# A decode step with a 65536-entry cache: the K and V chunks issued from another engine's queue

## The chip, the cores and the metric

The kernel runs on one core of a Trainium2 chip. The core has a matrix engine (TensorE, PE in the profile), a vector engine (VectorE, DVE), a scalar engine (ScalarE, ACT), GpSimd (POOL) and a sync engine (SyncE, SP) that mostly issues transfers. Sixteen DMA engines move data between HBM and the on-chip memory SBUF; PSUM holds TensorE's results. Engines wait for one another, and for transfers, through semaphores. The metric is device time in microseconds, as a median over runs; lower is better.

## What is computed

One token goes through a grouped-query attention block with a cache, and then a bilinear GLU. There are 32 query heads and 8 K/V heads, so four query heads share one K/V head. The cache has 65536 entries of 128 floats for each K/V head, once for K and once for V: 2 x 8 x 65536 x 128 floats of 4 bytes, 537 MB. Everything is float32.

```
q = layernorm(x) @ wq                       # (1, 32 x 128)
scores = q . k * 128**-0.5                  # per head, over 65536 entries
o = softmax(scores) . v
h = x + o @ wo                              # (1, 512)
n = layernorm(h)
out = h + ((n @ w_gate) * (n @ w_up)) @ w_down
```

## The kernel before

**Chunks.** The host lays K and V out as 64 chunks of 128 partitions x 16384 floats (8 MB each, `kvd[g]`). A K/V head has four K chunks and then four V chunks, so head h owns chunks 8h to 8h+7. SBUF has room for two: even chunks go into `kv[0]`, odd ones into `kv[1]`. The weights of a head (`wqo`: the query weights of the next head and the output weights of this one) have one buffer of their own, `wqo_sb`.

**TensorE.** `windows` multiplies a chunk in pieces of 512 columns (L364, 64 matmuls a chunk in the profile). It waits for the chunk's landing on a semaphore: `s_k0` for `kv[0]`, `s_v0` for `kv[1]`, each raised by 16 when a chunk has landed. The other semaphores of that kind (`s_k16`, `s_v8` and so on) exist for chunks that come in several pieces; GpSimd sets them to a high count at the start. When TensorE is done with a chunk it raises `kd`, and VectorE then raises `free` by one.

**SP's program.** All transfers of K, V and weights are issued by SP, in program order, on one queue. It loads the first query weights (L121), chunks 0 and 1, then chunks 2 to 5, each after taking one count of `free`. Then comes a loop over seven heads: take `wf` (VectorE says that the weights' buffer may be overwritten), issue the head's weights `wqo[h]` (L148), and then eight times take `free` and issue a chunk (`even`, L116, and `odd`, L119). After the loop come the last output weights `wo7` (L154), chunk 62, chunk 63 in four pieces (L160), and the GLU's weights (L163 to L172) into the two big buffers. The output is stored at L495.

**GpSimd** only prepares constants: an identity matrix, zeroed buffers, and the counts just named. Then it waits for the end of the program.

`take(e, s, n)` makes engine e wait until semaphore s has at least n and then takes n away.

```
    def even(g):
        sp.dma_start(kv[0], kvd[g]).then_inc(s_k0, 16)
    def odd(g):
        sp.dma_start(kv[1], kvd[g]).then_inc(s_v0, 16)
```

Of the kernel before, what the change touches and what calls it, by code (L numbers as in the profile page):

```python
# [13 lines left out]
NT = SK // CK  # L14
# [6 lines left out]
LAST = HKV - 1  # L21
PE_ONLY, DVE_ONLY, ACT_ONLY, SP_ONLY = (bass.OrderedEngineSet([e]) for e in (
    mybir.EngineType.PE, mybir.EngineType.DVE, mybir.EngineType.Activation, mybir.EngineType.SP))
# [7 lines left out]
class Counter:  # L31
# [5 lines left out]
    def tick(self, inst):  # L37
        self.n += 1
        inst.then_inc(self.sem, 1)
        return self.n  # L40


def body(nc, xr, kvd, wq0, wqo, wo7, gu, wd, out):
    pe_e, dve_e, act_e, pool_e, sp = nc.tensor, nc.vector, nc.scalar, nc.gpsimd, nc.sync

    def tile(name, *shape, align=32):
        return nc.alloc_sbuf_tensor(name, list(shape), F32, align_bytes=align).ap()
# [14 lines left out]
    kv = [tile(f"kv{i}", P, CK, align=1024) for i in range(2)]  # L62
    wqo_sb = tile("wqo_sb", P, 2, KT, 512, align=1024)
# [22 lines left out]
    def sem(name):  # L86
        sems.append(nc.alloc_semaphore(name))
        return sems[-1]
# [6 lines left out]
    pa, da, free, wf = (sem(n) for n in ("pa", "da", "free", "wf"))  # L95
    s_k0, s_k16, s_k24, s_k28 = (sem(f"s_k{i}") for i in (0, 16, 24, 28))
    s_v0, s_v8, s_v16, s_v24, s_v28 = (sem(f"s_v{i}") for i in (0, 8, 16, 24, 28))
    s_wq, s_w = sem("s_wq"), sem("s_w")
    s_wd = [sem(f"s_wd{i}") for i in range(NC - SIDE)]
    s_xr = sem("s_xr")  # L100
    late, s_act, s_pool, s_y, s_a, s_out = (sem(n) for n in ("late", "s_act", "s_pool", "s_y", "s_a", "s_out"))
    gu_t = kv[0].rearrange("p (k x) -> p k x", k=KT)[:, :, 0:2 * F]
    wd_t = kv[1]
# [2 lines left out]
    def take(e, s, n=1):  # L106
        e.wait_ge(s, n).then_inc(s, -n)  # L107
# [27 lines left out]
        pool_e.sem_inc(p, w * (end // 2 + n))  # L135
    for t in (o_pad, f_pad, sel_pad, acc, y):
        c_pads = pool.tick(pool_e.memset(t, 0.0))
    pool_e.wait_ge(s_act, 1).then_inc(s_pool, 1)
    pool_e.br("fin")

# [2 lines left out]
    for g in range(2, 6):  # L143
        take(sp, free)
        (odd if g % 2 else even)(g)
    with nc.Fori(0, LAST, engines=SP_ONLY) as h:
        take(sp, wf)
        sp.dma_start(wqo_sb, wqo[h]).then_inc(s_w, 16)  # L148
        with nc.Fori(0, 2 * NT, 2, engines=SP_ONLY) as c:
            for i, put in enumerate((even, odd)):  # L150
                take(sp, free)
                put(c + (h * (2 * NT) + 6 + i))
    take(sp, wf)
    sp.dma_start(wo_sb, wo7).then_inc(s_w, 16)  # L154
    take(sp, free)
# [175 lines left out]
    for o, g, u in ((f_pad[:, 0:1, 0], gux[0][:, 0, 3:4, 0], uf[:, 0, 1, 3:4, 0]),  # L331
                    (f_pad[:, 1:4, 0], gux[1][:, 1, 0:3, 0], uf[:, 1, 1, 0:3, 1]),
                    (f_pad[:, 4:5, 0], gux[1][:, 0, 3:4, 0], uf[:, 1, 1, 3:4, 0])):
        i = dve_e.scalar_tensor_tensor(
            out=o, in0=g, scalar=ln_r3[:, 0:1], in1=u, op0=ALU.mult, op1=ALU.mult)
# [17 lines left out]
    for k in range(KT):  # L353
        if k == KT - 1:
            pe_e.wait_ge(s_wq, 16)
        i = pe_e.transpose(ps[0][:, k:k + 1], xn_row[0:1, k * P:(k + 1) * P], ident[0:1, 0:1])
# [35 lines left out]
    for k in range(KT):  # L392
        i = mm(ptp[0][0:1, :], xn[:, k:k + 1], wq_sb[:, k, :], start=(k == 0), stop=(k == KT - 1))  # L393
    i.then_inc(pd, 1)
    pe_e.wait_ge(tok, 4)
    for r in range(REP):
        i = pe_e.transpose(sm[0][:, r:r + 1], qrow[0:1, r * P:(r + 1) * P], ident[0:1, 0:1])  # L397
# [13 lines left out]
    for half in range(2):  # L411
        pe_e.wait_ge(atok[half], 1)
        for b in range(4):
            i = pe_e.transpose(ptp[half][:, b * P:(b + 1) * P], ex[half][:, b * P:(b + 1) * P], ident)  # L414
# [9 lines left out]
    for half in range(2):  # L424
        step()
        for b in range(2):
            i = pe_e.transpose(ptp[half][:, b * P:(b + 1) * P],
                               gu_sb[:, (2 * half + b) * P:(2 * half + b + 1) * P], ident)
# [25 lines left out]
    for b in range(4):  # L454
        if b < 3:
            pe_e.wait_ge(*((tob, 1), (s_w, 16), (tob, 2))[b])
        i = pe_e.transpose(ptp[1][:, b * P:(b + 1) * P], orow[:, b * P:(b + 1) * P], ident)  # L457
    i.then_inc(pd, 1)
    pe_e.wait_ge(tok, 2)
    for r in range(REP):  # L460
        i = mm(attn[32 * r:32 * r + 32, :], o_pad[:, r, :], wo_sb[:, r, :],  # L461
               start=True, stop=True)
# [6 lines left out]
    for k in range(KT):  # L469
        if k % 2 == 0:  # L470
            pe_e.wait_ge(*((s_a, HKV) if k else (tok, 3)))
        i = pe_e.transpose(ptp[1][:, k * P:(k + 1) * P], acc[:, k * P:(k + 1) * P], ident)
# [69 lines left out]
```

## Time and profile before

| | |
|---|---|
| median of 3 runs | 1308.68 us (1308.65 to 1309.05) |
| span of the profiled execution, first to last instruction | 1307.4 us |
| median less that span | 1.3 us |
| TensorE matmuls, busy | 686.2 us (52%) |
| VectorE, busy | 111.6 us (9%) |
| ScalarE, busy | 54.9 us (4%) |
| GpSimd, busy | 2.7 us (12 instructions) |
| read from HBM | 564.66 MB |

The profile is of one execution. Busy times of different engines overlap, so they do not add up to the span. "Idle before" in a row is the time in which that engine stood still ahead of an instruction, with what ended the wait. Waiting and issuing a transfer are not counted as busy; a transfer's own time shows in the DMA rows. In a row of a timeline the first number is the start and the second the length, both in microseconds. PEld is the loading of weights into TensorE, and a name ending in q (SPq, DVEq) is an engine's instruction stream, where waits and issues stand.

### The profile page before, as it was taken

Reading aid. Unit: us, or ns where it says so; the run is one execution under the profiler, and the core shown is the slowest. Engines: PE = TensorE matmul, PEld = TensorE weight load, DVE = VectorE, ACT = ScalarE, POOL = GpSimd, SP = SyncE. Lnnn points to the kernel's source line nnn. Section 1 sums busy time; section 2 is a strip of 40 time slices with the busy share of each in tenths; the row PEclk is TensorE's granted clock in tenths of the full one; section 3 lists DMA queues with packets and bytes.
Section 4 is the critical chain, followed back from the end, with each engine's and each line's share of the span. In section 5 each row is a group of like instructions: output and inputs, shape, how many; then the busy total and the mean of one; then the engine's idle time right before and its main releaser. Section 6 shows DMA issues by size and latency. Waiting matters only on the chain. (4 is left out here: it accounts for less than half of the span.)

```text
span 1307.4 us, 10833 instructions
## 1 busy us (share of the span) xinstructions
PE 686.2 (52%) x4610; PEld 191.5 (15%) x4610; DVE 111.6 (9%) x286; ACT 54.9 (4%) x106; POOL 2.7 (0%) x12
## 2 busy tenths in 40 slices
PE   4456364453654545553554636535566445545557
PEld 1011111110111111111110211101111111111112
DVE  1000010100101001000010101001010010100101
ACT  0000000000000000000000000000000000000000
POOL 0000000000000000000000000000000000000000
PEclk8676796776976768767787767868677677877679
DMA  9999999999999999999999999999999999999999
GB/s 417 421 445 429 437 447 419 449 417 449 417 449 417 449 417 449 421 445 427 439 439 427 449 417 449 417 449 417 449 417 449 417 434 440 441 437 429 447 408 382
DMA packets 12850, 564.72 MB, mean 432 GB/s; under 512 B 1409, under 2 KB 1457, under 8 KB 2610
## 3 DMA queue, kind: packets, MB, share of 16 engines
q1 hardware_dynamic: 12848, 564.71, 99.8%
q10 hardware_dynamic: 2, 0.00, 0.0%
HBM read 564.66 MB, written 0.05 MB: 432 GB/s over the span
## 5 line engine op out<-in xcount | busy, mean ns | idle before, releaser
L364 PE MATMUL ps<-kv,st 128*32 128x512 f32 x4184 | 591.0, 728 | 534.6 <-DMA kv<-in_kv 520.1
L364 PEld LDWEIGHTS ps<-kv,st 128*32 128x32 f32 x4184 | 146.7, 131 | 962.3 <-DMA kv<-in_kv 568.1
L242 DVE TENSOR_REDUCE mx<-sc 128x1 f32<-128x512 f32 x32 | 21.9, 686 | 535.9 <-DVEq L107 535.9
L414 PE MATMUL ptp<-ident,ex 128*128 128x128 f32 x128 | 27.3, 372 | 19.8 <-ACT ex L220 19.5
L216 ACT COPY sc<-ps 128x512 f32<-128x512 f32 x32 | 18.8, 586 | 444.6 <-ACTq L107 444.5
L274 DVE TENSOR_TENSOR orow<-ps,orow 128x512 f32<-128x512 f32 x16 | 11.1, 691 | 298.3 <-DVEq L107 298.3
L220 ACT ACTIVATE ex<-sc,nbias 128x512 f32<-128x512 f32 x32 | 22.8, 714 | 304.4 <-ACTq L107 304.4
L393 PE MATMUL ptp<-wqo_sb,xn 128*1 128x512 f32 x64 | 30.4, 620 | 6.4 <-DVE acc L288 5.0
L216 ACT ACT_TABLE_LOAD x8 | 10.3, 1283 | 441.5 <-ACTq L107 441.5
L261 DVE COPY st<-ptp 128x512 f32<-128x512 f32 x32 | 22.1, 692 | 44.5 <-DVEq L107 44.5
L414 PEld LDWEIGHTS ptp<-ident,ex 128*128 128x128 f32 x128 | 20.2, 188 | 22.9 <-ACT ex L220 22.8
L407 PE MATMUL sm<-ident,m 128*1 128x128 f32 x16 | 4.5, 283 | 27.2 <-DVE m L244 17.6
L277 DVE TENSOR_TENSOR orow<-ps,orow 128x256 f32<-128x256 f32 x16 | 6.0, 419 | 129.3 <-DVEq L107 129.3
L272 DVE COPY orow<-ps 128x512 f32<-128x512 f32 x8 | 5.5, 692 | 102.0 <-DVEq L107 102.0
L461 PE MATMUL attn<-wqo_sb,o_pad 128*32 128x512 f32 x64 | 8.5, 605 | 5.9 <-DVE o_pad L284 5.9
L409 PE MATMUL sm<-ones,mexp 1*128 1x1 f32 x32 | 6.9, 281 | 6.7 <-DVE mexp L251 6.7
L393 PEld LDWEIGHTS ptp<-wqo_sb,xn 128*1 128x1 f32 x64 | 4.9, 85 | 30.9 <-issue 18.1
L224 DVE COPY qrow<-ptp 1x512 f32<-1x512 f32 x8 | 5.4, 679 | 29.7 <-DVEq L107 29.7
L457 PE MATMUL ptp<-ident,orow 128*128 128x128 f32 x32 | 6.1, 300 | 3.0 <-DVE orow L277 3.0
L407 PEld LDWEIGHTS sm<-ident,m 128*1 128x1 f32 x16 | 1.3, 79 | 41.8 <-DVE m L244 24.9
L288 DVE SCALAR_TENSOR_TENSOR acc<-attn,acc 128x256 f32<-128x256 f32 x16 | 6.2, 421 | 10.8 <-DVEq L107 10.8
L397 PE MATMUL sm<-ident,qrow 1*128 1x1 f32 x32 | 3.2, 201 | 7.1 <-DVE qrow L224 7.1
(84 smaller groups left out, 78.4 us busy)
## 6 DMA issues: line engine op xcount, KB each, us to landing
wqo_sb<-in_wqo SPq DMA_DIRECT2D x7, 2048.0 KB, 32.9
kv<-in_kv SPq DMA_DIRECT2D x1, 4096.0 KB, 22.2
kv<-in_gu SPq DMA_DIRECT2D x1, 3584.0 KB, 17.6
kv<-in_kv SPq DMA_DIRECT2D x1, 2048.0 KB, 26.7
kv<-in_kv SPq DMA_DIRECT2D x2, 1024.0 KB, 29.7
kv<-in_gu SPq DMA_DIRECT2D x1, 1792.0 KB, 21.4
kv<-in_wd SPq DMA_DIRECT2D x1, 1536.0 KB, 19.0
kv<-in_wd SPq DMA_DIRECT2D x5, 256.0 KB, 20.5
```

The source lines that it names most:

```text
L216: act_e.copy(sc[s], ps[s % 2]).then_inc(ad, 1)
L220: act_e.activation(ex[s - n], sc[s], AF.Exp, bias=nbias[:, 0:1], scale=SCALE, accum_out=sums[:, s:s + 1]).then_inc(atok[s - n], 1)
L242: dve_e.tensor_reduce(out=mx[:, s:s + 1], in_=sc[s], axis=AX.X, op=ALU.max).then_inc(own, 1)
L261: dve_e.tensor_copy(st[:, :, 0:16].rearrange("p g (b h) -> p b g h", h=REP), ptp[n % 2].rearrange("p (b g h) -> p b g h", b=4, h=REP)).the ...
L274: mine(dve_e.tensor_tensor(out=orow, in0=ps[n % 2], in1=orow, op=ALU.add))
L288: dve_e.scalar_tensor_tensor(out=acc[:, cs], in0=attn[:, cs], scalar=1.0, in1=acc[:, cs], op0=ALU.mult, op1=ALU.add, accum_out=rsum[:, hal ...
L364: i = mm(ps[buf][32 * j:32 * j + 32, :], st[:, 8 * j + r, :], kv[buf][:, w * 512:(w + 1) * 512], start=(r == 0), stop=(r in (2, 3, 7)), sk ...
L393: i = mm(ptp[0][0:1, :], xn[:, k:k + 1], wq_sb[:, k, :], start=(k == 0), stop=(k == KT - 1))
L409: mm(sm[0][:, 0:1], mexp.rearrange("p g h -> p (g h)"), ones[0:1, 0:1], start=True, stop=True).then_inc(pd, 1)
L414: i = pe_e.transpose(ptp[half][:, b * P:(b + 1) * P], ex[half][:, b * P:(b + 1) * P], ident)
L457: i = pe_e.transpose(ptp[1][:, b * P:(b + 1) * P], orow[:, b * P:(b + 1) * P], ident)
L461: i = mm(attn[32 * r:32 * r + 32, :], o_pad[:, r, :], wo_sb[:, r, :], start=True, stop=True)
```

## The change

Of the 64 chunks, numbers 6 to 61 are now issued by GpSimd in a loop of its own. GpSimd starts after SP has issued chunk 5 and raised a new semaphore `go`; it takes `free` before every chunk, as SP did. A chunk's landing no longer raises the semaphore on which TensorE waits: it raises `landed[0]` or `landed[1]`, and SP waits for that count and then raises `s_k0` or `s_v0` by 16 itself. SP's loop is written out in full, 56 steps long, with the weights `wqo[h]` issued at every eighth step. The last output weights, chunks 62 and 63 and the GLU's weights stay with SP, behind the 56 steps.

```
+POOL_ONLY = bass.OrderedEngineSet([mybir.EngineType.Pool])
...
+    go = sem("go")
+    landed = [sem(f"landed{i}") for i in range(2)]
...
         c_pads = pool.tick(pool_e.memset(t, 0.0))
+    take(pool_e, go)
+    with nc.Fori(0, LAST, engines=POOL_ONLY) as h:
+        with nc.Fori(0, 2 * NT, 2, engines=POOL_ONLY) as c:
+            for i, (buf, p) in enumerate(zip(kv, landed)):
+                take(pool_e, free)
+                pool_e.dma_start(buf, kvd[c + (h * (2 * NT) + 6 + i)]).then_inc(p, 16)
     pool_e.wait_ge(s_act, 1).then_inc(s_pool, 1)
...
     for g in range(2, 6):
         take(sp, free)
         (odd if g % 2 else even)(g)
-    with nc.Fori(0, LAST, engines=SP_ONLY) as h:
-        take(sp, wf)
-        sp.dma_start(wqo_sb, wqo[h]).then_inc(s_w, 16)
-        with nc.Fori(0, 2 * NT, 2, engines=SP_ONLY) as c:
-            for i, put in enumerate((even, odd)):
-                take(sp, free)
-                put(c + (h * (2 * NT) + 6 + i))
+    sp.sem_inc(go, 1)
+    for g in range(6, 2 * NT * LAST + 6):
+        n = (g - 6) // 2 + 1
+        if g % 8 == 6:
+            take(sp, wf)
+            sp.dma_start(wqo_sb, wqo[g // 8]).then_inc(s_w, 16)
+        sp.wait_ge(landed[g % 2], 16 * n)
+        sp.sem_inc(s_v0 if g % 2 else s_k0, 16)
     take(sp, wf)
     sp.dma_start(wo_sb, wo7).then_inc(s_w, 16)
```

Below, the rows of an engine's instruction stream give the code line, the operation and, in brackets, the semaphores for which it waits. First SP before the change, from the last two loads ahead of the loop to chunk 63 (the loop's body begins behind the two branches; what is left out is its second half and the jumps back):

```order
L116 DMA kv<-in_kv 128x16384 [waits free]
L119 DMA kv<-in_kv 128x16384 [waits free]
L146 UNCONDITIONAL_BRANCH
L148 ISA [waits wf]
L148 DMA wqo_sb<-in_wqo 128x4096
L149 UNCONDITIONAL_BRANCH
L116 ISA [waits free]
L116 DMA kv<-in_kv 128x16384
...
L154 DMA wqo_sb<-in_wo 128x2048 [waits wf]
L116 DMA kv<-in_kv 128x16384 [waits free]
L160 DMA kv<-in_kv 128x8192 [waits free]
```

The same place in SP's stream after the change (the lines are numbered anew; L162 is the former L148, L166 the former L154):

```order
L121 DMA kv<-in_kv 128x16384 [waits free]
L124 DMA kv<-in_kv 128x16384 [waits free]
L162 DMA wqo_sb<-in_wqo 128x4096 [waits wf]
L162 DMA wqo_sb<-in_wqo 128x4096 [waits landed0,landed1,wf] x6
L166 DMA wqo_sb<-in_wo 128x2048 [waits landed0,landed1,wf]
L121 DMA kv<-in_kv 128x16384 [waits free]
L172 DMA kv<-in_kv 128x8192 [waits free]
```

The loop's chunks are gone from SP. Its seven loads of `wqo` stand in a row; the first has no landing ahead of it, the other six, and the load of `wo7` at L166 with chunk 62 behind it, stand behind waits for landings. Now GpSimd's stream after the change, from its last memset to its last wait:

```order
L142 MEMSET y 128x256
L144 UNCONDITIONAL_BRANCH [waits go]
L145 UNCONDITIONAL_BRANCH
L148 ISA [waits free]
L148 DMA kv<-in_kv 128x16384
L148 ISA [waits free]
L148 DMA kv<-in_kv 128x16384
L145 REGISTER_ALU
L145 COMPARE_AND_BRANCH
L144 REGISTER_ALU
L144 COMPARE_AND_BRANCH
L150 UNCONDITIONAL_BRANCH [waits s_act]
```

Before, the last memset was followed at once by the wait for the end (`s_act`); now two nested loops with two chunks a turn stand between them, each chunk behind one count of `free`.

## What I expect, and why

> **What bounds the kernel now.** I read the queue table first, then one long stretch of the transfers, then the waits, and last the timeline where work changes hands.
>
> ```profile
> q1 hardware_dynamic: 12848, 564.71, 99.8%
> DMA packets 9552, 511.71 MB, mean 434 GB/s; under 512 B 1072, under 2 KB 1072, under 8 KB 1072
> PEld ps L364 <- DMA kv<-in_kv: 568.1, 63, 13.0
> SPq L107 <- SPq L107: 1225.3, 66, 32.5
> ```
>
> The first line is the page's: one queue carries all the data, and its packets fill 99.8% of the time of the sixteen DMA engines. The second is the stretch from 20 to 1200 us, at a steady 434 GB/s. A chunk of 128x16384 floats (8.39 MB) therefore takes 8.39/434 = 19.3 us. The other two are waits: TensorE waits 568 us for chunks, and the sync engine (SP) 1225 us, nearly all of it for free buffers. Compute has time to spare; the end is set by bytes and by any moment in which the DMA engines have nothing queued. There is almost none today, so the 0.2% that is left (2.6 us) is all that better queueing could win.
>
> ```profile
> 54.52 0.33 SPq L119 DMA_DIRECT2D kv<-in_kv  x1
> 44.26 9.96 PE L364 MATMUL ps<-kv,st 128*32 128x512 f32 x64 [9.95 <-DMA kv<-in_kv]
> 993.33 0.33 SPq L116 DMA_DIRECT2D kv<-in_kv  x1
> 1000.94 2.79 PE L364 MATMUL ps<-kv,st 128*32 128x512 f32 x12 [8.14 <-DMA kv<-in_kv]
> ```
>
> This is why the queue never empties. A chunk that TensorE takes up at 44.26 is worked through by 54.2, and the next load into its buffer is issued at 54.52. The chunk already in flight needs 19.3 us from 44, so the new one stands in the queue about 9 us before it is needed. The second pair shows the thinnest place that I found: the issue at 993.33, and the chunk ahead of it taken up at 1000.94. So every issue has a **cushion** of at least 7 us.
>
> **The change part by part.**
>
> *The relay.* SP now sees a landing and hands TensorE the count: 56 times one wait and one increment.
>
> ```profile
> L107 SPq EVENT_SEMAPHORE  x74: 17/17/17, 34.6 to 1307.4; - x74
> 1305.37 0.42 DVE L492 COPY y<-pva 64x256 f32<-64x256 f32 x1 [1.78 <-PE pva L374]
> 1305.81 0.36 SPq L495 DMA_DIRECT2D out_y<-y  x1
> ```
>
> SP's semaphore instructions take 17 ns, and SP issues the output within 0.1 us of the end of the copy that releases it. I take 0.1 us per chunk, between 0.03 us (two instructions) and 0.3 us (from TensorE's end at 54.22 through VectorE to SP's issue at 54.52, two steps, in the rows above). TensorE starts, and frees its buffer, that much later; the 7 us cushion hides it. Without the cushion it would cost 56 x 0.1 = 6 us.
>
> *GpSimd's issue.* Its queue never carried data before, so its time from free buffer to first byte has no row. Below it is bounded by nothing, above by the 2.4 us that a load into an empty queue costs (worked out below); I take 1 us. The cushion hides either end. GpSimd's older work ends with the memset below at 3.46 us, so nothing stands behind its new waits except its last step at the end of the program.
>
> ```profile
> 3.14 0.32 POOL L137 MEMSET y<- 128x256 f32 x1
> L234 DVE COPY st<-qx x8: 693/694/695, 16.5 to 1140.2; 128x1024 f32<-128x1024 f32 x8
> ```
>
> Eight VectorE copies from SBUF to SBUF take 0.69 us each. The Trainium skill (SBUF — State Buffer, "SBUF: two separate sides") warns that GpSimd cannot write a transfer's descriptors while such a copy holds the port that they share. By that rule an estimate of at most 8 x 0.69 = 5.5 us of late issues would be added; the cushion of 7 us makes it nothing, and no run here shows it yet.
>
> *The rate on GpSimd's queue.* Unknown. Below: no gain, since packets already stand back to back. Above: if each of the 56 chunks exposed its whole start, 56 x 2.4 = 134 us. Between these, if the queue cuts the 64 KB rows smaller, the tail of the trace has prices for it.
>
> ```profile
> DMA packets 160, 8.65 MB, mean 433 GB/s; under 512 B 16, under 2 KB 16, under 8 KB 16
> DMA packets 279, 1.60 MB, mean 422 GB/s; under 512 B 18, under 2 KB 18, under 8 KB 279
> DMA packets 491, 0.89 MB, mean 405 GB/s; under 512 B 56, under 2 KB 56, under 8 KB 491
> ```
>
> These are three stretches: 125 to 145 us (whole rows of K and V), 1295.2 to 1299 (pieces of 6 KB), 1301.3 to 1303.5 (2 KB). Beside each count stand the small completion packets. At 422 GB/s a chunk takes 19.9 us, 0.55 more, x56 = 31 us; at 405 GB/s 20.7, 1.4 more, 78 us. I take no loss, because the nearest row is the chunk itself, whose shape and addresses do not change.
>
> The Trainium skill (DMA: Bandwidth & Descriptors, "Bandwidth", the measured table) gives 425 GB/s for 16 MB issued from GpSimd. An estimate by that figure is 19.74 us a chunk, 0.4 more, and a total near 1335 us; no run here shows it yet.
>
> *The first handover, chunk 5 to chunk 6.* SP's queue still holds chunk 5 and, behind it, the weights of L148, issued at 93.38, when GpSimd issues chunk 6 at about 113 into a queue of its own. From there two queues share the engines.
>
> ```profile
> 93.38 0.35 SPq L148 DMA_DIRECT2D wqo_sb<-in_wqo  x1
> 112.79 0.34 SPq L116 DMA_DIRECT2D kv<-in_kv  x1
> 121.65 4.94 PE L364 MATMUL ps<-kv,st 128*32 128x512 f32 x25 [9.40 <-DMA kv<-in_kv]
> 130.97 0.33 SPq L119 DMA_DIRECT2D kv<-in_kv  x1
> 145.87 1.94 PE L364 MATMUL ps<-kv,st 128*32 128x512 f32 x8 [11.12 <-DMA kv<-in_kv]
> ```
>
> Chunk 5 has some 8 us of data left at 113. Shared evenly it lands near 129 instead of 121.3, and its buffer is free about 9.3 us after (121.65 to 130.97), near 139. Chunk 5, the weights and chunk 6 together still end at 145.5, so chunk 7 is issued in time: no cost. Sharing never creates bytes; it costs only if something then runs dry.
>
> *The weights of the later heads.* SP issues them only after the landing of the sixth of eight chunks, beside one that GpSimd has already queued. They take 2.10 MB/434 = 4.8 us of DMA time as before, and the head's end, which needs them, is still two chunks (over 38 us) away: no cost.
>
> *The last handover, chunk 61 to 62.* Here is the one term that I count. SP issues the last weights (L154) and then chunk 62, until now far ahead:
>
> ```profile
> 1209.71 0.34 SPq L154 DMA_DIRECT2D wqo_sb<-in_wo  x1
> 1228.65 0.34 SPq L116 DMA_DIRECT2D kv<-in_kv  x1
> 1237.59 6.77 PE L364 MATMUL ps<-kv,st 128*32 128x512 f32 x44 [9.26 <-DMA kv<-in_kv]
> 1259.42 3.63 PE L364 MATMUL ps<-kv,st 128*32 128x512 f32 x15 [8.62 <-DMA kv<-in_kv]
> ```
>
> Chunk 61 is taken up at 1237.59, chunk 62 at 1259.42. Before, both issues were made by 1229. Now SP stands in front of them waiting for chunk 61's landing, and everything behind that wait on SP (the weights, chunks 62 and 63, the GLU weights) is late. GpSimd has nothing more to issue, so all queues are empty at that landing. What a load into an empty queue costs, the first and the last one show:
>
> ```profile
> wqo_sb<-in_wq SPq DMA_DIRECT2D x1, 1024.0 KB, 4.8
> wqo_sb<-in_wo SPq DMA_DIRECT2D x1, 1024.0 KB, 30.3
> out_y<-y SPq DMA_DIRECT2D x1, 48.0 KB, 1.6
> ```
>
> The program's first load, 1024 KB, needs 4.8 us, of which 1.05 MB/434 = 2.4 is transfer: **2.4 us** of start and landing. The output, 48 KB, has 1.6 - 0.1 = 1.5 us. The load in question is the first one's size and also comes from HBM, so I take 2.4, with 1.5 as the lower end; SP's semaphore steps add 0.1, at most 0.3. All that follows is one chain of transfers to the end, so the whole of it, **2.5 us** (1.6 to 2.7), arrives there.
>
> ```profile
> span 1307.4 us, 10833 instructions
> 1280.60 18.98 DMA kv<-in_wd
> ```
>
> *Sum.* Span 1307.4 + 2.5 = 1309.9. The median of the runs, 1308.68, lies 1.3 above that span; with the same 1.3 around it the forecast is 1311.2 us, 0.19% slower. The chain's last transfer, the second line, only moves.
>
> **The rivals.**
>
> *GpSimd's queue is slower per chunk* (slower overall). Place: each of 56 chunks; price: 0.1 us each makes 5.6 us, 6 KB pieces 31 us, with the handover 1317 to 1342; at 2 KB pieces or an exposed start, up to 1445. It decides as soon as a chunk's time exceeds 19.3 us. For it: no row of before shows this queue moving data. Against it: the same rows, buffers and addresses, and 7 us in which an issue can be prepared. Chance 0.27, of which 0.07 lies above 1342. An extreme of it, a chunk at half the rate, would add 56 x 19.3 = 1081 us: 2392 us, chance 0.03. The microseconds column of the skill's measured table just named (79.0 for 16 MB) would mean about that, against its own GB/s column.
>
> *The queues share unevenly at the first handover* (slower). If chunk 6 goes first, chunk 5 lands at 121.3 + 19.3 = 140.6, its buffer is free at 150, and all queued data has ended at 145.5: idle from there to 150 plus about 2 us of start, 6.5 us, total 1317.7. It decides once chunk 5 lands after about 134. Nothing shows an order between queues; chance 0.06.
>
> *The last handover costs less, or the change does not do what it says* (same). If the next load starts almost at once, or some load is still queued at that landing, the total is 1308.7 to 1310. For it: SP reacts in 0.1 us. Against: even the tiny output needs 1.6 us. Chance 0.07; 0.02 of that I give to a gain past 0.2%, for which packets would have to run faster than 434 GB/s.
>
> **How the numbers follow.** The forecast (only the last handover counts, 1310.2 to 1312.5) has 0.57. The measurement tells about 0.2% from no change, so the border is 1311.3, and the forecast lies right on it: 0.33 below, 0.24 above. Same: 0.33 + 0.05 = 0.38; slower: 0.24 + 0.27 + 0.03 + 0.06 = 0.60; faster 0.02. The range runs from 1308.7 (a free handover) to 1342 (6 KB pieces), leaving out about 0.12; the forecast's own is 1310.2 to 1312.5.
>
> **What would show it.** In the queue table of the changed kernel a second queue carries about 56 x 8.39 = 470 MB; over the middle heads the rate stays 434 GB/s, and a chunk is taken up every 19.3 us. A lower rate there, or more packets than 128 a chunk, is the first rival. Chunk 5 is taken up near 129 instead of 121.65; after 134 is the second. After chunk 61's take-up a gap of about 2 us without packets stands before L166's weights, and chunk 62 is taken up 2.5 us later than 1259.42. Idle DMA stretches anywhere else, or a GpSimd issue less than 1 us before it is needed, would prove the cushion argument wrong.

## The result, and the profile after

The changed kernel takes **1311.81 us** (median of 11 runs, 1311.59 to 1312.03) against 1308.73 us for the kernel before (11 runs): ratio 1.0023, 95% interval 1.0014 to 1.0032. It is 3.1 us slower. The profiled execution has a span of 1310.7 us, 3.3 above that of before.

First the page of the changed kernel: its span, its queues, and the wait that took the place of TensorE's wait for transfers. Then the stretch from 20 to 1200 us.

```profile
span 1310.7 us, 10877 instructions
q0 software_dynamic: 8064, 469.77, 82.7%
q1 hardware_dynamic: 4784, 94.95, 16.9%
q14 instruction: 1, 0.01, 0.0%
PEld ps L376 <- SPq L164: 499.4, 55, 13.0
DMA packets 9553, 511.72 MB, mean 434 GB/s; under 512 B 1072, under 2 KB 1072, under 8 KB 1072
```

A second queue, q0, now carries 469.77 MB, which is the 56 chunks. The packets are as large and as many as before (9553 against 9552 in the same stretch), and the rate is the same 434 GB/s. The one packet more is on q14, an instruction fetch. TensorE now waits for SP's relay (L164) instead of the transfers, but hardly longer: 499.4/55 = 9.1 us a time, where before it was 568.1/63 = 9.0, and at most 13.0 as before.

The time is lost at the last handover. The timeline of the changed kernel shows TensorE taking up chunks 61 and 62, with SP's issues between them; the fifth line is the transfers of the stretch from 1237.75 to 1239.2, and the last line the weights' time from issue to landing.

```profile
1238.15 8.71 PE L376 MATMUL ps<-kv,st 128*32 128x512 f32 x64 [9.47 <-SPq L164]
1238.24 0.33 SPq L166 DMA_DIRECT2D wqo_sb<-in_wo  x1
1238.69 0.35 SPq L121 DMA_DIRECT2D kv<-in_kv  x1
1262.33 1.93 PE L376 MATMUL ps<-kv,st 128*32 128x512 f32 x8 [11.19 <-DMA kv<-in_kv]
DMA packets 3, 0.02 MB, mean 17 GB/s; under 512 B 0, under 2 KB 0, under 8 KB 0
wqo_sb<-in_wo SPq DMA_DIRECT2D x1, 1024.0 KB, 4.7
```

The weights, issued 30.3 us ahead of their landing before, now take 4.7 us: they start into an empty queue, and 1.45 us pass with 3 packets in them. From chunk 61 to chunk 62 it is 1262.33 - 1238.15 = 24.18 us; before it was 1259.42 - 1237.59 = 21.83. The difference is **2.35 us**.

Of all executions behind this document one, of the run early62 below, fell in a slow state (1425.69 us) and is left out of that run's ratio.

### The profile page after: what moved, and what is told of

Read it like the earlier page. It is cut to its first block, busy times and chain, and to the rows that moved or that the text cites. A ratio compares the mean times of both kernels' runs of the same rounds, so it can differ in the third digit from the quotient of the medians.

```text
span 1310.7 us, 10877 instructions
## 1 busy us (share of the span) xinstructions
PE 685.5 (52%) x4610; PEld 192.0 (15%) x4610; DVE 111.5 (9%) x286; ACT 54.9 (4%) x106; POOL 32.4 (2%) x68
## 3 DMA queue, kind: packets, MB, share of 16 engines
q0 software_dynamic: 8064, 469.77, 82.7%
## 5 line engine op out<-in xcount | busy, mean ns | idle before, releaser
L376 PE MATMUL ps<-kv,st 128*32 128x512 f32 x4184 | 589.4, 726 | 538.4 <-SPq L164 455.8
L376 PEld LDWEIGHTS ps<-kv,st 128*32 128x32 f32 x4184 | 146.2, 130 | 965.2 <-SPq L164 499.4
L148 POOL DMA_DIRECT2D kv<-in_kv x56 | 29.7, 530 | 1177.1 <-POOLq L112 1177.1
L426 PE MATMUL ptp<-ident,ex 128*128 128x128 f32 x128 | 28.5, 387 | 19.7 <-ACT ex L232 19.5
L273 DVE COPY st<-ptp 128x512 f32<-128x512 f32 x32 | 22.1, 692 | 45.2 <-DVEq L112 45.2
## 6 DMA issues: line engine op xcount, KB each, us to landing
kv<-in_gu SPq DMA_DIRECT2D x1, 1792.0 KB, 23.2
```

The lines of the kernel that those rows point to most:

```text
L148: pool_e.dma_start(buf, kvd[c + (h * (2 * NT) + 6 + i)]).then_inc(p, 16)
L273: dve_e.tensor_copy(st[:, :, 0:16].rearrange("p g (b h) -> p b g h", h=REP), ptp[n % 2].rearrange("p (b g h) -> p b g h", b=4, h=REP)).the ...
L376: i = mm(ps[buf][32 * j:32 * j + 32, :], st[:, 8 * j + r, :], kv[buf][:, w * 512:(w + 1) * 512], start=(r == 0), stop=(r in (2, 3, 7)), sk ...
```

## Experiments

All are edits of one of the two kernels; each was timed beside the kernel before on the same chip.

| run | median, us | before, us | ratio, 95% interval |
|---|---|---|---|
| early62 | 1309.10 | 1308.84 | 1.0003 (0.9994 to 1.0011) |
| sp_relay | 1308.86 | 1308.84 | 1.0001 (0.9992 to 1.0010) |
| slow_relay | 1400.15 | 1308.84 | 1.0694 (1.0679 to 1.0710) |
| slow_relay_8 | 1316.23 | 1308.77 | 1.0056 (1.0040 to 1.0073) |
| second_gap | 1316.05 | 1308.84 | 1.0055 (1.0042 to 1.0068) |
| pool_one_at_a_time | 1506.56 | 1308.77 | 1.1512 (1.1493 to 1.1531) |
| sp_one_at_a_time | 1483.56 | 1308.77 | 1.1335 (1.1316 to 1.1354) |

**Fill the queue at the last handover (early62).** The first line stands behind GpSimd's loop, the rest in SP's.

```
+    pool_e.sem_inc(gone, 1)
...
         if g % 8 == 6:
             take(sp, wf)
             sp.dma_start(wqo_sb, wqo[g // 8]).then_inc(s_w, 16)
+        if g == 2 * NT * LAST + 5:
+            take(sp, wf)
+            sp.dma_start(wo_sb, wo7).then_inc(s_w, 16)
+            take(sp, gone)
+            take(sp, free)
+            even(end - 2)
         sp.wait_ge(landed[g % 2], 16 * n)
         sp.sem_inc(s_v0 if g % 2 else s_k0, 16)
-    take(sp, wf)
-    sp.dma_start(wo_sb, wo7).then_inc(s_w, 16)
-    take(sp, free)
-    even(end - 2)
```

> The changed kernel, but SP issues the last output weights and chunk 62 before it waits for chunk 61's landing (GpSimd tells SP when its loop is done, so that SP takes the right count of `free`). Theory (the empty queue at the last handover is the cost, 2.4 us in the changed kernel's trace): 1311.8 - 2.4 = 1309.4 us, and chunk 62's data follows chunk 61's without a pause. Rival (the relay or GpSimd's queue costs a little on each of the 56 chunks): 1311.8 us, as the change.

Measured: 1309.10 us; 2.7 us of the 3.1 are gone, and the interval includes no difference from before. SP's timeline in this run shows the two issues far ahead of the landing, and TensorE's shows the take-ups of chunks 61 and 62:

```profile
1218.93 0.33 SPq L166 DMA_DIRECT2D wqo_sb<-in_wo  x1
1228.59 0.33 SPq L121 DMA_DIRECT2D kv<-in_kv  x1
1240.29 8.94 PE L379 MATMUL ps<-kv,st 128*32 128x512 f32 x64 [12.01 <-SPq L171]
1259.85 2.79 PE L379 MATMUL ps<-kv,st 128*32 128x512 f32 x12 [6.34 <-DMA kv<-in_kv]
```

Chunk 61 is taken up 2.1 us later than in the change (1240.29 after 1238.15): the last weights, issued by SP at 1218.93, now share the engines with it, and nearly all of their 2.4 us of transfer comes ahead of its landing instead of behind it. Chunk 62 is taken up at 1259.85, 0.4 us later than before the change instead of 2.9. Relay and GpSimd's queue are as in the change, so they are not the cost; the empty queue is.

**The relay alone (sp_relay).** SP issues every chunk as before, on its own queue.

```
-    for g in range(2, 6):
+    for g in range(2, 5):
         take(sp, free)
         (odd if g % 2 else even)(g)
+    take(sp, free)
+    sp.dma_start(kv[1], kvd[5]).then_inc(landed[1], 16)
...
+    def relay(i):
+        take(sp, landed[i], 16)
+        sp.sem_inc((s_k0, s_v0)[i], 16)
...
-            for i, put in enumerate((even, odd)):
+            for i in range(2):
                 take(sp, free)
-                put(c + (h * (2 * NT) + 6 + i))
+                sp.dma_start(kv[i], kvd[c + (h * (2 * NT) + 6 + i)]).then_inc(landed[i], 16)
+                relay(1 - i)
...
     even(end - 2)
+    relay(1)
```

> The kernel before with the relay alone: SP still issues every chunk, but chunks 5 to 61 raise a semaphore of SP's, and SP hands TensorE the count, always after it has issued the next chunk. No GpSimd queue, no empty queue. Theory (the relay is hidden by the cushion): 1308.7 to 1309.0 us. Rival (the relay is the cost): 1311.8 us.

Measured: 1308.86 us, no difference. A relay behind a filled queue costs nothing here.

**A longer relay (slow_relay, 24 turns; slow_relay_8, 8 turns).** A turn raises and takes a semaphore that nobody else uses.

```
         sp.wait_ge(landed[g % 2], 16 * n)
+        with nc.Fori(0, 24, engines=SP_ONLY):
+            sp.sem_inc(slack, 1)
+            take(sp, slack)
         sp.sem_inc(s_v0 if g % 2 else s_k0, 16)
```

> The changed kernel with each relay made longer: 24 turns of an empty loop on SP between the landing and the count, by estimate 2 to 4 us. Theory (hidden by the cushion of some 7 us; paid once, at the last handover, where nothing is queued): the change plus one delay, 1314 to 1316 us. Rival (each relay is paid): 56 delays, 110 to 220 us more, 1420 to 1540 us.

Neither number came: 1400.15 us. My estimate of the loop, which stood on no row of a trace, was wrong. Between a landing at 570.87 (the last completion packet of that chunk in the trace) and the take-up at 580.46 lie 9.6 us. In its timeline:

```profile
580.46 9.65 PE L379 MATMUL ps<-kv,st 128*32 128x512 f32 x64 [10.43 <-SPq L167]
591.13 0.53 POOL L148 DMA_DIRECT2D kv<-in_kv  x1 [19.57 <-POOLq L112]
602.48 8.88 PE L379 MATMUL ps<-kv,st 128*32 128x512 f32 x64 [12.38 <-SPq L167]
```

The next chunk's take-up comes 22.0 us later instead of 19.3. The delay is longer than many of the cushions: here GpSimd issues a chunk at 571.04, 0.2 us after that landing, into an empty queue. The loss, less the one delay of 9.2 us at the last handover, is (1400.15 - 1311.81 - 9.2)/55 = 1.4 us a chunk: far from 9.2, so most of each delay was still hidden. The run bounds the cushion from above (in the change 31 of GpSimd's 55 issues behind its first have less than 9.2 us), and a third of the turns was the better test:

> The changed kernel with each relay longer by 8 turns of the empty loop instead of 24. The 24 turns took about 9.2 us between a chunk's landing (570.87) and TensorE's take-up (580.46), more than the cushion; 8 turns should take 3.1 us, within it. Theory: hidden for 55 chunks and paid once at the last handover, 1311.8 + 3.1 = 1314.9 us. Rival (a relay costs in proportion at every chunk): a third of what 24 turns cost, 1311.8 + 29 = 1341 us.

Measured: 1316.23 us. The rival's 1341 is excluded: 55 of 56 delays are hidden, and one is paid at the handover, where the take-up comes 3.5 us behind chunk 61's last completion packet (1242.61 after 1239.10) and not 0.4 us (1238.15 after 1237.71) as in the change. It is 1.3 us above my number. In the trace chunk 61 already lands 1.4 us later than in the change; this longer program has three packets on the instruction queue instead of one (see the last section). The trace of the changed kernel gives the cushion itself: the smallest distance from an issue of GpSimd's to the landing of the chunk ahead is 7.0 us (137.51 to 144.47), and the next smallest 7.9 (973.59 to 981.45).

**A second empty queue (second_gap).**

```
+    for lo, hi in ((6, 32), (32, 62)):
+        if lo > 6:
+            take(pool_e, mid)
+        with nc.Fori(lo, hi, 2, engines=POOL_ONLY) as c:
...
         sp.sem_inc(s_v0 if g % 2 else s_k0, 16)
+        if g == 31:
+            sp.sem_inc(mid, 1)
```

> The changed kernel with a second handover of the same kind: GpSimd issues chunk 32 only after SP has seen chunk 31's landing, so all queues are empty once more. Theory (an empty queue costs its start and landing): 2.4 to 3.0 us more, 1314.2 to 1314.8 us, with a pause of about 2 us without packets after chunk 31. Rival (the change's cost is spread over the chunks, or one pause is absorbed): 1311.8 us.

Measured: 1316.05 us, 4.2 us more than the change: the effect is there and the rival falls, but it is half as large again as expected. The timeline of this run, and its transfers from 643.1 to 645.8:

```profile
643.54 9.70 PE L380 MATMUL ps<-kv,st 128*32 128x512 f32 x64 [10.50 <-SPq L166]
644.49 0.53 POOL L150 DMA_DIRECT2D kv<-in_kv  x1 [33.70 <-POOLq L112]
666.72 8.36 PE L380 MATMUL ps<-kv,st 128*32 128x512 f32 x64 [4.60 <-SPq L166]
686.19 4.14 PE L380 MATMUL ps<-kv,st 128*32 128x512 f32 x20 [11.11 <-SPq L166]
DMA packets 7, 0.39 MB, mean 146 GB/s; under 512 B 1, under 2 KB 1, under 8 KB 1
```

From chunk 31 to 32 it is 23.2 us instead of 19.3: the pause costs 3.9 us, 2.6 of them with no packet, and the next chunks are a little slow too (686.19 - 666.72 = 19.5). So this start on GpSimd's queue is dearer than the 2.35 us on SP's. Two more kernels ask whether that is the queue or the size of the load.

**One chunk at a time, on either queue.** First GpSimd waits for each landing (SP raises `nxt` behind each relay); then SP does the same on its own queue, in the kernel of sp_relay.

```
                 take(pool_e, free)
+                take(pool_e, nxt)
                 pool_e.dma_start(buf, kvd[c + (h * (2 * NT) + 6 + i)]).then_inc(p, 16)
```

> The changed kernel with the cushion taken away: GpSimd issues chunks 7 to 61 only after SP has seen the landing of the chunk before, so the price of an issue into an empty queue of GpSimd's shows 55 times. Theory: 3.9 us each, as at the one pause of the run with the second handover (landing to landing 23.2 instead of 19.3 us): about +200 to 215 us, 1512 to 1527 us. Rival (that pause was dear because it came once, the usual price is SP's 2.4 us): +132 us, 1444 us.

```
                 sp.dma_start(kv[i], kvd[c + (h * (2 * NT) + 6 + i)]).then_inc(landed[i], 16)
-                relay(1 - i)
+                relay(i)
```

> The kernel before, with SP issuing chunks 6 to 61 on its own queue, each only after the landing of the chunk before (SP waits for it and hands TensorE the count). No GpSimd queue. Theory: 2.4 us for each of the 56 starts into an empty queue, 1308.7 + 134 = 1443 us; it tells the price of SP's queue from GpSimd's. Rival (both queues cost the same): the same excess as the GpSimd run of this call.

Measured: 1506.56 and 1483.56 us. Per start, from one landing to the next, that is (1506.56 - 1311.81)/55 = 3.5 us on GpSimd's queue and (1483.56 - 1308.77)/56 = 3.1 us on SP's. The take-ups with one issue between them, first GpSimd's kernel, then SP's:

```profile
213.37 9.17 PE L380 MATMUL ps<-kv,st 128*32 128x512 f32 x64 [14.21 <-SPq L166]
214.18 0.53 POOL L149 DMA_DIRECT2D kv<-in_kv  x1 [22.36 <-POOLq L112]
236.47 9.56 PE L380 MATMUL ps<-kv,st 128*32 128x512 f32 x64 [13.94 <-SPq L166]
```

```profile
213.04 9.66 PE L370 MATMUL ps<-kv,st 128*32 128x512 f32 x64 [13.39 <-SPq L149]
213.68 0.33 SPq L157 DMA_DIRECT2D kv<-in_kv  x1
235.63 8.61 PE L370 MATMUL ps<-kv,st 128*32 128x512 f32 x64 [12.93 <-SPq L149]
257.73 5.20 PE L370 MATMUL ps<-kv,st 128*32 128x512 f32 x21 [13.50 <-SPq L149]
```

A chunk takes 23.1 us there and 22.6 and 22.1 here, against 19.3 with a filled queue. Both stated prices were off, SP's more: I had priced it by the 1 MB load. But the size makes little of the difference. These are the two kernels' issues between 20 and 1200 us, SP's first, with the median from issue to landing at the end of the row:

```profile
kv<-in_kv SPq DMA_DIRECT2D x51, 21.8
kv<-in_kv POOLq DMA_DIRECT2D x47, 22.1
```

Beyond the 19.3 us of transfer that is 2.5 us on SP's queue and 2.8 on GpSimd's, where the 1 MB of weights at the last handover had 4.7 - 2.4 = 2.3. The rest is the issuing engine's way from a landing to its next issue: SP issues 0.64 us after the take-up (213.68 after 213.04) or 0.27 (235.90 after 235.63), GpSimd 0.81 (214.18 after 213.37), and SP at the last handover 0.09 (1238.24 after 1238.15). So an 8 MB chunk into an empty queue costs about 3 us in SP's loop, and GpSimd's adds some 0.4 us. These are the starts that the cushion hides 55 times in the changed kernel.

## Why the prediction was right, and where it was off

The forecast was 1311.2 us with 2.5 us at one place; the time is 1311.81.

- **The bound and the rate.** The rate on GpSimd's queue is the same 434 GB/s, with 64 KB rows. The rival of a slower queue falls, and so does the estimate of 1335 us by the measured table of the Trainium skill (DMA: Bandwidth & Descriptors, "Bandwidth").
- **The relay.** Estimated 0.1 us. Counted from a chunk's last completion packet in the trace, the take-up came 0.36 us later before (24.92 after 24.56, chunk 0) and 0.44 us later in the change (1238.15 after 1237.71, chunk 61): 0.1 us, as estimated. That it is hidden is shown by sp_relay and, lengthened by 3 us, by slow_relay_8.
- **GpSimd's issue.** Hidden, as said: nothing runs dry over 1100 us. Every issue stands at least 7.0 us ahead of its need, far from the 1 us that would have proved the cushion wrong. What I took as 1 us to the first byte can be seen where each engine issues one chunk at a time: the first packet starts 1.2 us after GpSimd's issue (215.4 after 214.18), and 1.0 us after SP's (214.6 after 213.68). The estimate by the Trainium skill's rule on the shared port (SBUF — State Buffer, "SBUF: two separate sides"), up to 5.5 us from VectorE's copies, is not in the time, but the rule was not put to the test either: no such copy runs near an issue of GpSimd's.

```profile
175.68 0.53 POOL L148 DMA_DIRECT2D kv<-in_kv  x1 [20.04 <-POOLq L112]
184.21 0.69 DVE L246 COPY st<-qx 128x1024 f32<-128x1024 f32 x1
193.14 0.53 POOL L148 DMA_DIRECT2D kv<-in_kv  x1 [16.93 <-POOLq L112]
```

The copy stands 8.5 us behind one issue and 8.9 us ahead of the next; the six after it are as far from any issue, and the first, at 16.68, comes before GpSimd issues at all.

- **The first handover.** Mechanism right, numbers off. GpSimd issues chunk 6 at 113.56, and until 118.4 all packets are still SP's. From there the two queues take turns, a packet of 64 KB on each of the sixteen engines. The rows with q1 (SP's) and q0 (GpSimd's) are what one queue moved in each of five stretches of 2.4 us, one after the other from 115.4 to 127.4; in the last, where GpSimd's again moved 16 packets, SP's are the 16 completion packets of chunk 5.

```profile
113.56 0.67 POOL L148 DMA_DIRECT2D kv<-in_kv  x1 [109.99 <-POOLq L112]
q1 hardware_dynamic: 16, 1.05, 100.8%
q0 software_dynamic: 16, 1.05, 100.8%
q1 hardware_dynamic: 16, 1.05, 100.8%
q0 software_dynamic: 16, 1.05, 100.8%
q1 hardware_dynamic: 16, 0.00, 0.4%
126.72 9.76 PE L376 MATMUL ps<-kv,st 128*32 128x512 f32 x64 [14.30 <-DMA kv<-in_kv]
165.39 4.91 PE L376 MATMUL ps<-kv,st 128*32 128x512 f32 x24 [11.31 <-SPq L164]
```

Two turns of GpSimd's, 4.8 us, came ahead of chunk 5's landing. It is taken up at 126.72, not near 129, because the sharing began 5 us later than I took it; chunk 7 at 165.39, against 165.15 before, which is the 0.2 us of the start (below). The take-up stays far from the 134 from which it would have cost anything. So the rival of uneven sharing falls, and with it its premise: packets of equal size took equal turns.

- **The last handover.** Predicted 2.4 + 0.1, of which the relay's 0.1 already lies ahead of chunk 61's take-up; measured 2.35 behind it. early62 shows it as the cause: the same kernel with this queue filled is level with before.
- **What the sum lacked.** 0.8 us of the profile's 3.3. Chunk 61 is taken up 0.56 later than before (the relay's 0.1 is in it), and after chunk 62 another 0.35 is lost:

```profile
24.92 5.53 PE L364 MATMUL ps<-kv,st 128*32 128x512 f32 x28 [9.20 <-DMA kv<-in_kv]
25.12 5.07 PE L376 MATMUL ps<-kv,st 128*32 128x512 f32 x24 [9.19 <-DMA kv<-in_kv]
1287.36 3.64 PE L364 MATMUL ps<-kv,st 128*32 128x512 f32 x32 [2.26 <-DMA kv<-in_gu]
1290.62 9.78 PE L376 MATMUL ps<-kv,st 128*32 128x512 f32 x64 [2.85 <-DMA kv<-in_gu]
```

L364 is the kernel before, L376 the changed one. Of the 0.56, 0.2 is there from chunk 0 on. Another 0.3 comes near 1150 us, with an instruction fetch (see the last section). The 0.35 is the growth from 1262.33 - 1259.42 = 2.91 to 1290.62 - 1287.36 = 3.26. It is absent in early62, whose first GLU take-up is at 1287.81, no later against before than its chunk 62. It goes with the handover's pause: from the last completion packet of chunk 63's first piece to that of the first GLU weights it is 18.28 us before, in sp_relay and in early62, and 18.5 to 18.6 in the change and in the five other runs, which all have the pause. By which step, no run shows.

## What to carry to other kernels

Where a transfer queue was always filled, neither the issuing engine nor a relay of its landings mattered here, up to the distance between an issue and the moment when its data could start: 3.1 us of delay were hidden, 9.2 not wholly. What mattered is every place where an engine waits for a landing ahead of the next issue: look there for an issue that is still outstanding, and if there is none, put one ahead of the wait. One such place cost 2.35 to 3.9 us here; up to 0.9 us of that range is the time that the issuing engine took from the take-up to its next issue (0.09 us at the last handover, 0.95 in second_gap).

## What was not expected

**Instruction fetches on the DMA engines.** SP's loop is written out in the change, and the program fetches once more while it runs. The first two rows are the take-ups around it in the kernel before, the next two in the change, and the last is the change's stretch from 1140.8 to 1160.5:

```profile
1141.03 8.77 PE L364 MATMUL ps<-kv,st 128*32 128x512 f32 x64 [1.59 <-DMA kv<-in_kv]
1160.31 10.01 PE L364 MATMUL ps<-kv,st 128*32 128x512 f32 x64 [10.51 <-DMA kv<-in_kv]
1141.27 8.77 PE L376 MATMUL ps<-kv,st 128*32 128x512 f32 x64 [1.65 <-SPq L164]
1160.98 9.74 PE L376 MATMUL ps<-kv,st 128*32 128x512 f32 x64 [10.94 <-SPq L164]
q14 instruction: 1, 0.01, 0.1%
```

The chunk takes 19.7 us with the fetch and 19.3 without. early62 has the same fetch at the same place and the same loss, slow_relay_8 has three fetches and lands its chunk 61 1.4 us late; but the fetch of second_gap at 1130 us lengthened no chunk. That one DMA engine, held up by the fetch, makes the whole chunk late is my reading, and the sixteen completion packets of a chunk agree with it. In the change the first of them comes 19.32 us after that of the chunk before, as without a fetch, and the last 19.59; from first to last it is 0.62 us ahead of the fetch and 0.89 behind it. In slow_relay_8 the same spread grows at each of the three fetches (0.45 to 0.74, 0.78 to 1.33, 1.33 to 1.92); in second_gap it stays at 0.6. No run took the fetch away alone.

**Turns by packet, not by bytes.** At the first handover the two queues took turns packet by packet. That is even only while their packets are of one size: from 127.4 to 130.8 us, beside the weights' packets of 16 KB, each queue again moved 16 packets, but GpSimd's 1.05 MB and SP's 0.26. It was seen at the first handover of the change and was not tested by itself.
